# The first words tile on GpSimd's queue, in two halves, and decoded in front of the first exponentials

## The chip, the cores and the metric

The kernel runs on one core of one Trainium2 chip. The core has a TensorE (PE: matmuls, and the weight loads in front of them, PEld), a VectorE (DVE), a ScalarE (ACT), a GpSimd (POOL) and a SyncE (SP), which share the on-chip memory SBUF; matmuls write to PSUM. Transfers between HBM and SBUF are asked for by an engine's queue (here SP's, once ACT's) and carried by 16 DMA engines that the core's queues share. The metric is device time in microseconds. The kernel before took 1014.36 us, the median of three runs (1013.2 to 1014.84).

## The reference

Four batches of eight heads of attention with a threshold: a score below the row's maximum minus tau is dropped before the softmax. Its output goes through two feed-forward nets: the first is gated and has no nonlinearity but the product, the second has a leaky ReLU.

```
scores = q @ k.T / 8                                   # 4 x 8 heads, 576 x 576, head_dim 64
attn   = softmax(where(scores >= max(scores) - tau, scores, -1e9))
x = (attn @ v) -> 2304 x 512                           # heads side by side
x = ((x @ w1) * (x @ w2)) @ w3 @ w_out                 # w1, w2: 512 x 1024; w3: 1024 x 1024; w_out: 1024 x 512
h = x @ w_in                                           # 512 x 2048
out = maximum(0.01 * h, h) @ moe2_w_out                # 2048 x 512
```

All inputs are float32 of small magnitude.

## The kernel before

The weights reach the core as 64-bit words, whose two 32-bit columns (`low` and `high`) make one float32 value; a *half* is 512 such values in each of 128 partitions. Decoding a half (`decode`, lines 137 to 161) takes two activations on ACT (L147 on the high words into `t`, L149 on the low words into `lw`), a shift on DVE (L150) and two additions on POOL (L154). Halves that belong to w1 and w2 are also split in two parts, which takes an ACT cast (L156) and a subtraction (L158, on DVE for every second half). There are 40 halves: those of w_out and w3 come in pairs, one 1 MB transfer to a `raw` tile for two halves (L133), those of w1 and w2 singly (L127, `st`). The order is `first` (lines 406 and 407): w_out's tiles 0 and 1, w3's tile 0, w_out's 2 and 3, and so on. Called h0, h1, ... here, h0 and h1 are the first `raw` tile, h2 and h3 the second, h4 and h5 (w3's tile 0) the third, h6 and h7 the fourth.

The attention runs over 80 steps (`STEPS`). One step is a block of 128 query rows of two heads, or of 64 rows of each: `scores` (PE matmuls L262, then on DVE the negated row maximum L271 and on ACT the exponentials L272), `mask` (DVE L286, the sum's reciprocal L290 and L291, and in the first three steps a diagonal `dg` of the reciprocals, L295 on ACT and L296 on DVE), `transposes` (PE L314 or L312, copies L355 on ACT and L347 on DVE) and, once per head pair, `weighted` (PE L371, the product with V). Q is scaled in `prepare_unit` (DVE, L216) before the first scores of its head pair. Into these steps the program lays the decoding (`load_halves`), the product of w3 and w_out that is taken once (`fold_weights`, PE L420, in pieces of two matmuls given out by `fold_some`), and later, as filler on PE, the first net for the 384 tokens that are finished (`gated`, L450 and L471). The second net follows as a pure matmul stage (L909, L944).

PE's and SP's instructions stay in the order in which the program is written; ACT's, DVE's and POOL's are ordered by a scheduler that may move them, except those under `keep_in_program_order`, to which the two activations of a decode and the scaling of Q belong. Every engine works through its own list and stops at an instruction that waits. Before the first scores PE multiplies the identity with itself nine times, and ten times behind them (`keep_busy`, L527), which keeps it running until there is work; the identity is made by POOL (masks.py, lines 197 and 199).

At the start SP asks for the first head pair's K and Q (four transfers, L186 and L190), for h0 and h1 (L133), for the second pair's K and Q, for the next three `raw` tiles, and for V (L202, L203). In step 0 the program decodes h0 before `mask(0)` and h1 after its transposes, in steps 1 to 4 four halves each. The transfer of a further `raw` tile waits for one of four buffers.

Of the kernel before, what the change touches and what calls it, by code (L numbers as in the profile page):

```python
# [10 lines left out]
I32 = mybir.dt.int32  # L11
# [38 lines left out]
def attention_gated_ffn(ctx: ExitStack, tc: tile.TileContext, qkv, tau, w3t, wout, w12, w2, out):  # L50
# [6 lines left out]
    nc = tc.nc  # L57

    def f(ap):
        return ap.bitcast(F32)  # L60
# [44 lines left out]
    def stream(jobs, by_dve):  # L105

        todo = [(job, c) for job in jobs for c in range(2)]
        loaded = []
        state = [0, None]

        def issue(most=2 * len(jobs)):

            while len(loaded) < min(most, len(todo)):
                (slot, src, raw), c = todo[len(loaded)]
                if len(loaded) >= state[0] + (7 if raw else 5):
                    return
                if raw is None:
                    st = wld.tile([P, 1024], I32, tag="st", name="st", bufs=4)
                    nc.sync.dma_start(out=st, in_=src[:, c * 512:c * 512 + 512].bitcast(I32))  # L127
                    loaded.append(st)
                else:
                    if c == 0:  # L130
                        state[1] = wpool.tile(
                            [P, 2, 1024], I32, tag=raw, name="raw")
                        nc.sync.dma_start(  # L133
                            out=state[1].rearrange("p c w -> p (c w)"), in_=src.bitcast(I32))
                    loaded.append(state[1][:, c])

        def decode():
            for k, ((slot, src, raw), c) in enumerate(todo):
                if c == 0:
                    dst = slot()  # L140
                sl = slice(c * 512, c * 512 + 512)
                words = loaded[k].rearrange("p (w two) -> p w two", two=2)
                low, high = words[:, :, 0], words[:, :, 1]
                t = wld.tile([P, 512], I32, tag="t", name="t", bufs=2)
                lw = wld.tile([P, 512], I32, tag="lw", name="lw", bufs=2)
                tc.keep_in_program_order(
                    nc.scalar.activation(f(t), f(high), AF.Prelu, scale=2.0 ** -112, alpha=-2.0 ** 32))  # L147
                tc.keep_in_program_order(
                    nc.scalar.activation(lw, low.bitcast(U32), AF.Copy, scale=2.0 ** -29))  # L149
                nc.vector.tensor_scalar(  # L150
                    out=t, in0=t, scalar1=3, scalar2=None, op0=ALU.logical_shift_left)
                whole = dst[:, sl].bitcast(I32) if len(dst.shape) == 2 else lw
                for part in (slice(0, 256), slice(256, 512)):
                    nc.gpsimd.tensor_tensor(out=whole[:, part], in0=t[:, part], in1=lw[:, part], op=ALU.add)  # L154
                if len(dst.shape) == 3:
                    nc.scalar.copy(dst[:, 0, sl], f(t))  # L156
                    eng = nc.vector if by_dve and c else nc.gpsimd
                    eng.tensor_tensor(out=dst[:, 1, sl], in0=f(lw), in1=f(dst[:, 0, sl]), op=ALU.subtract)  # L158
                state[0] = k + 1
                yield  # L160
                issue()

        return decode(), issue
# [3 lines left out]
    def piece_of(u):  # L167

        b, p, g = UNITS[u]
        gq, gw, blocks = PARTS[b % 2][g]  # L170
        at = b * S + gq
        return gq, gw, blocks[0] is None, at // GW, at % GW

    def load_unit(u):

        if u >= len(UNITS):
            return
        b, p, _ = UNITS[u]
        gq, gw, _, _, _ = piece_of(u)
        h = 2 * p  # L180
        qk = apool.tile([P, KS + GW], F32, tag="qk", name="qk", bufs=3)
        for a in range(2):
            o = a * D
            src = qkv[b, h + a][o:o + D]
            if gq == 0:
                nc.sync.dma_start(out=qk[o:o + D, D:KS + gw], in_=src[:, :S + gw])  # L186
            else:
                nc.sync.dma_start(out=qk[o:o + D, D:KS], in_=src[:, :S])
                nc.sync.dma_start(out=qk[o:o + D, KS:KS + gw], in_=src[:, S + gq:2 * S])
            nc.sync.dma_start(out=qk[o:o + D, :D], in_=src[:, S - D:S])  # L190
        qk_t[u] = qk
# [49 lines left out]
    def scores(n, between=None):  # L241

        u, c = STEPS[n]
        qk = qk_t[u]
        heads = range(1 if c is None else 2)
        sc = [ps_a.tile([P, 2, 512], F32, tag=f"sc{a}", name="sc") for a in heads]
        if u < PER:
            parts, qzu = (qk,), qz.unsqueeze(1)
        else:
            parts, qzu = qks_t[u], qzs  # L250
        passes = PASSES[:1] if u < PER else PASSES
        for half in range(2):
            for i, (x, y) in enumerate(passes):
                for a in heads:
                    if c is None:
                        lhs, rhs = qzu[:, x], parts[y][:, D + half * HS:D + half * HS + HS]
                    else:
                        r = slice(a * D, a * D + D)
                        o = KS + c
                        k0 = (D, 0)[a] + half * HS  # L260
                        lhs, rhs = parts[x][r, o:o + P], parts[y][r, k0:k0 + HS]
                    nc.tensor.matmul(  # L262
                        sc[a][:, half, :HS], lhs, rhs, start=(i == 0), stop=(i == len(passes) - 1))
        if between:
            between()
        e = apool.tile([P, 2 * S], F32, tag="e", name="e", bufs=2)
        few = apool.tile([P, 6], F32, tag="nm", name="nm", bufs=4)
        nms, th = few[:, :2], few[:, 2:4]
        for a in heads:
            nm = nms[:, a:a + 1]  # L270
            nc.vector.tensor_reduce(out=nm, in_=sc[a][:, :, :HS], op=ALU.max, axis=AX.XY, negate=True)  # L271
            ex = nc.scalar.activation(  # L272
                e[:, a * S:a * S + S].rearrange("p (a b) -> p a b", a=2), sc[a][:, :, :HS], AF.Exp, bias=nm)
            if between:
                tc.keep_in_program_order(ex)
        m = len(heads)
        nc.vector.tensor_scalar(
            out=th[:, :m], in0=nms[:, :m], scalar1=-1.0, scalar2=cb, op0=ALU.mult, op1=ALU.add)
        sc_t[n], e_t[n] = (sc, [th[:, a:a + 1] for a in heads], few[:, 4:]), e
# [110 lines left out]
    def slot(table, i, tag, name):  # L390
        def make():
            if tag == "w3":
                table[i] = fold.tile([P, 1024], F32, tag=tag, name=name, bufs=3)
            elif name == "wo":
                if i % 2 == 0:
                    table["both"] = fold.tile([P, 2, 1024], F32, tag=tag, name=name, bufs=2)
                table[i] = table["both"][:, i % 2]
            else:
                table[i] = wpool.tile([P, 2, 1024], F32R, tag=tag, name=name)
            return table[i]  # L400
        return make
# [87 lines left out]
    in_order = ExitStack()  # L489
    in_order.enter_context(tc.manual_schedule(engines={mybir.EngineType.SP}))  # L490
    load_tau()
    load_unit(0)
    loads, issue = stream(first, True)
    issue(2)
    load_unit(1)
    issue()
    load_v(0)
    prepare_unit(0)
    halves_in = [0]
    folded = [0]  # L500

    def load_halves(k):
        for _ in range(k):
            if next(loads, 0) != 0:
                halves_in[0] += 1
# [17 lines left out]
    def keep_busy(k):  # L523

        scratch = ps_w.tile([P, 512], F32, tag="w", name="scratch")
        for _ in range(k):
            nc.tensor.matmul(scratch[:, :P], ident, ident, start=True, stop=True)  # L527

    folding = fold_weights()
    keep_busy(9)  # L530
    scores(0)
    keep_busy(10)
    weigh = []
# [9 lines left out]
    for n in range(NS):  # L543
        u, c = STEPS[n]
# [106 lines left out]
    def issue():  # L651
        while len(raws) < min(used[0] + 3, len(order)):
            j, c = order[len(raws)]
            st = wld.tile([P, 1024], I32, tag="st", name="st", bufs=4)
            nc.sync.dma_start(out=st, in_=w2[j, :, c * 512:c * 512 + 512].bitcast(I32))
            raws.append(st)
# [387 lines left out]
```

## Time and profile before

| | |
|---|---|
| median of three runs | 1014.36 us |
| the profiled execution, its time | 1013.22 us |
| its span, first to last instruction | 1011.3 us |
| TensorE busy | 997.3 us (99%) |
| VectorE busy | 638.8 us (63%) |
| ScalarE busy | 571.3 us (56%) |
| GpSimd busy | 242.5 us (24%) |

The span is 1.9 us shorter than the execution's own time, and that is 1.14 us under the median. TensorE is busy nearly throughout, so what it stands idle for adds to the time. The page's second part cuts the span into 40 slices of 25 us; the whole change lies in the first of them and its consequences in the first six.

### The profile page before, as it was taken

What the parts mean: (1) busy time and instruction counts of PE and PEld (TensorE: products, weight loads), DVE (VectorE), ACT (ScalarE), POOL (GpSimd) and SP (SyncE); (2) the same over time, 40 slices, a digit from 0 to 9 for tenths busy, and PEclk for the clock granted to TensorE, in tenths of its full rate; (3) what the DMA queues carried; (4) which work ended last, traced back from release to release, by engine and by line L of the source; (5) the groups of instructions that cost most, each with busy time, mean ns of one, the idle gap of its engine ahead of it and who ended that gap; (6) DMA issues with size and microseconds to landing.
All of it is one profiled execution on the core that took longest, in us unless ns stands there. A gap on an engine that the chain in (4) does not pass through costs nothing.

```text
span 1011.3 us, 16227 instructions
## 1 busy us (share of the span) xinstructions
PE 997.3 (99%) x5909; PEld 846.8 (84%) x5909; DVE 638.8 (63%) x1370; ACT 571.3 (56%) x1068; POOL 242.5 (24%) x257
## 2 busy tenths in 40 slices
PE   7999999999999999999999999999999999999998
PEld 6544578888888888888888899999989999999997
DVE  7988889887777677898877355567582111521112
ACT  5978755555655554555655354878864333543332
POOL 2755531101100110111011062454461111411110
PEclk9999999999999999999999999999999999999999
DMA  8962422141121111223101227497537951074401
GB/s 263 344 220 98 129 58 58 53 131 34 34 64 49 40 30 62 59 71 88 45 12 55 68 88 273 176 326 265 173 130 278 392 213 42 1 282 160 192 1 63
DMA packets 52271, 129.51 MB, mean 128 GB/s; under 512 B 15712, under 2 KB 30304, under 8 KB 48352
## 3 DMA queue, kind: packets, MB, share of 16 engines
q1 hardware_dynamic: 51904, 128.35, 36.7%
q8 instruction: 47, 0.77, 0.3%
q14 instruction: 32, 0.26, 0.1%
q10 hardware_dynamic: 288, 0.13, 0.0%
HBM read 95.95 MB, written 32.51 MB: 127 GB/s over the span
## 4 chain that ended last, share of the span: by engine, by line
PE 85%; DVE 9%; ACT 3%; issue 2%; DMA 1%; POOL 0%; SPq 0%; DVEq 0%; ACTq 0%; POOLq 0%
PE po L944 19%; PE psab L450 18%; PE ps L909 17%; PE psh L471 10%; PE av L371 7%; PE sc L262 6%; PE tp L312 5%; PE ps L420 3%; DVE e L286 2%; DVE nm L271 2%; DMA qk<-in_qkv 1%; DVE t L150 1%; DVE HH L347 1%; DVE e L302 1%; PE tq L312 1%
## 5 line engine op out<-in xcount | busy, mean ns | idle before, releaser
L450 PE MATMUL psab<-x,w 128*128 128x384 f32 x1152 | 234.1, 347 | 0.0
L944 PE MATMUL po<-dn,gg 128*128 128x512 f32 x864 | 222.8, 390 | 0.0
L450 PEld LDWEIGHTS psab<-x,w 128*128 128x128 f32 x1152 | 196.4, 188 | 9.7 <-issue 9.4
L944 PEld LDWEIGHTS po<-dn,gg 128*128 128x128 f32 x864 | 160.0, 188 | 22.0
L909 PE MATMUL ps<-h,uph 128*128 128x384 f32 x672 | 172.8, 338 | 1.1 <-DVE sum L891 0.6
L891 DVE TENSOR_TENSOR sum<-snap,ps 128x384 f32<-128x384 f32 x72 | 39.8, 552 | 172.3 <-PE ps L909 156.5
L909 PEld LDWEIGHTS ps<-h,uph 128*128 128x128 f32 x672 | 123.5, 188 | 15.1 <-DVE sum L891 1.4
L272 ACT ACTIVATE e<-sc,nm 128x576 f32<-128x576 f32 x144 | 100.6, 739 | 62.7 <-DVE nm L271 62.1
L286 DVE SCALAR_TENSOR_TENSOR e<-sc,nm,e 128x576 f32<-128x576 f32 x144 | 113.1, 815 | 12.9 <-ACT e L272 7.9
L271 DVE TENSOR_REDUCE nm<-sc 128x1 f32<-128x576 f32 x144 | 103.3, 751 | 28.1 <-PE sc L262 28.0
L464 POOL TENSOR_TENSOR gt<-at,gt 128x384 fp32r<-128x384 f32 x46 | 47.5, 1033 | 299.4 <-ACT gt L462 299.4
L471 PE MATMUL psh<-gt,w 128*128 128x384 f32 x576 | 116.0, 346 | 0.0
L909 PE MATMUL ps<-h,upl 128*128 128x384 f32 x336 | 113.1, 337 | 0.0
L899 POOL TENSOR_TENSOR gg<-sum,gg 128x384 fp32r<-128x384 f32 x48 | 50.4, 1049 | 251.8 <-ACT gg L898 237.5
L471 PEld LDWEIGHTS psh<-gt,w 128*128 128x128 f32 x576 | 98.3, 188 | 6.3 <-issue 6.3
L886 ACT COPY snap<-ps 128x384 f32<-128x384 f32 x72 | 34.3, 476 | 89.4 <-PE ps L909 89.4
L312 PE MATMUL tp<-ident,e 128*128 128x128 f32 x488 | 73.8, 274 | 0.9 <-ACT HH L355 0.2
L312 PEld LDWEIGHTS tp<-ident,e 128*128 128x128 f32 x488 | 59.5, 140 | 17.5 <-issue 7.2
L371 PE MATMUL av<-HH,vv 128*64 128x384 f32 (+1 forms) x512 | 67.7, 407 | 0.5 <-DVE HH L347 0.5
L347 DVE COPY HH<-tp 128x512 f32<-128x512 f32 x64 | 43.7, 683 | 36.3 <-PE tp L312 36.1
L896 ACT ACTIVATE sum<-sum 128x384 f32<-128x384 f32 x72 | 37.8, 526 | 48.2 <-DVE sum L891 48.2
L909 PEld LDWEIGHTS ps<-h,upl 128*128 128x128 f32 x336 | 63.1, 188 | 0.0
(125 smaller groups left out, 1419.2 us busy)
## 6 DMA issues: line engine op xcount, KB each, us to landing
st<-in_w SPq DMA_DIRECT2D x48, 512.0 KB, 5.0
dn<-dn_d SPq DMA_DIRECT2D x10, 1024.0 KB, 7.2
uph<-up_d SPq DMA_DIRECT2D x10, 896.0 KB, 8.9
upl<-up_d SPq DMA_DIRECT2D x10, 896.0 KB, 4.7
raw<-in_w3t SPq DMA_DIRECT2D x8, 1024.0 KB, 9.6
vv<-in_qkv SPq DMA_DIRECT2D x64, 128.0 KB, 2.2
dn_d<-dn SPq DMA_DIRECT2D x8, 1024.0 KB, 6.5
up_d<-uph SPq DMA_DIRECT2D x8, 896.0 KB, 4.7
```

Source lines behind the costliest of these rows:

```text
L262: nc.tensor.matmul(sc[a][:, half, :HS], lhs, rhs, start=(i == 0), stop=(i == len(passes) - 1))
L271: nc.vector.tensor_reduce(out=nm, in_=sc[a][:, :, :HS], op=ALU.max, axis=AX.XY, negate=True)
L272: ex = nc.scalar.activation(e[:, a * S:a * S + S].rearrange("p (a b) -> p a b", a=2), sc[a][:, :, :HS], AF.Exp, bias=nm)
L286: nc.vector.scalar_tensor_tensor(out=ev, in0=sc[a][:, :, :HS], scalar=th, in1=ev, op0=ALU.is_ge, op1=ALU.mult, accum_out=st[:, a:a + 1])
L312: nc.tensor.transpose(out, part, ident)
L347: nc.vector.tensor_copy(HH[:, :, a, o:o + P], tp)
L371: nc.tensor.matmul(av[a * D:a * D + D, :gw], vv[:, a, kc], rhs, start=(i == 0), stop=(i == NK - 1))
L450: nc.tensor.matmul(ps, w12_t[i][:, a, mat * 512 + kk * P:mat * 512 + kk * P + P], xt[kk][:, c], start=(m == 0), stop=(m == 11))
L471: nc.tensor.matmul(ps, w34_t[i // 2][:, a, i % 2, o * P:o * P + P], gt[i][:, c], start=(m == 0), stop=(m == 23))
L899: eng.tensor_tensor(out=gg[:, 1], in0=gf, in1=f(gg[:, 0]), op=ALU.subtract)
L909: nc.tensor.matmul(ps, (uph, upl)[a][:, wi, i * P:i * P + P], hs[k][:, c, i], start=(opens[k] and m == 0), stop=(m == 5), skip_group_check ...
L944: nc.tensor.matmul(po_t[o], gg[:, c, t * P:t * P + P], dn[:, i, a], start=(q == 0 and seen[o] == 1 and m == 0), stop=(q == NQ - 1 and seen ...
```

## The change

The first `raw` tile (h0 and h1, 1 MB) is no longer asked for by SP in one transfer but by POOL in two of 512 KB each, and at the head of its program: `issue(2)` stands in front of `load_unit(0)`. Two halves are decoded (`load_halves(2)`) between the nine and the ten identity products, ahead of the first scores in the program. From there the decoding is two halves ahead of what it was at each place, with as many halves per step as before.

```diff
@@ in stream(), issue() @@
                     if c == 0:
                         state[1] = wpool.tile(
                             [P, 2, 1024], I32, tag=raw, name="raw")
-                        nc.sync.dma_start(
-                            out=state[1].rearrange("p c w -> p (c w)"), in_=src.bitcast(I32))
+                        words = src.bitcast(I32)
+                        if loaded:
+                            nc.sync.dma_start(out=state[1].rearrange("p c w -> p (c w)"), in_=words)
+                        else:
+                            for i in range(2):
+                                nc.gpsimd.dma_start(out=state[1][:, i], in_=words[:, i * 1024:i * 1024 + 1024])
@@ the start of the program @@
     load_tau()
-    load_unit(0)
     loads, issue = stream(first, True)
     issue(2)
+    load_unit(0)
     load_unit(1)
     issue()
     load_v(0)
...
     keep_busy(9)
+    load_halves(2)
     scores(0)
     keep_busy(10)
```

The lines of the changed kernel are four to five higher from `decode` on: its L151, L153, L154 and L158 are the L147, L149, L150 and L154 of before, its L220 is L216, L276 is L272, L299 is L295.

DVE at the start of the program, before: `scl` and `cb` come from tau, `qk` is Q, `sc` the scores, `t` the shifted words.

```order
L102 TENSOR_TENSOR cb<-cb,neg 128x1
L216 TENSOR_SCALAR qk<-qk,scl 128x384
L271 TENSOR_REDUCE nm<-sc 128x1 x2
L277 TENSOR_SCALAR nm<-nm,cb 128x2
L286 SCALAR_TENSOR_TENSOR e,nm<-sc,nm,e 128x576 x2
L150 TENSOR_SCALAR t<-t 128x512
L290 TENSOR_SCALAR nm<-nm 128x2
L291 RECIPROCAL nm<-nm 128x2
L296 TENSOR_SCALAR dg<-ident,nm 128x128
```

The same place on DVE in the changed kernel:

```order
L102 TENSOR_TENSOR cb<-cb,neg 128x1
L154 TENSOR_SCALAR t<-t 128x512
L220 TENSOR_SCALAR qk<-qk,scl 128x384
L154 TENSOR_SCALAR t<-t 128x512
L275 TENSOR_REDUCE nm<-sc 128x1 x2
L281 TENSOR_SCALAR nm<-nm,cb 128x2
L290 SCALAR_TENSOR_TENSOR e,nm<-sc,nm,e 128x576 x2
L154 TENSOR_SCALAR t<-t 128x512
L294 TENSOR_SCALAR nm<-nm 128x2
L295 RECIPROCAL nm<-nm 128x2
L300 TENSOR_SCALAR dg<-ident,nm 128x128
```

The shift of h0 now stands in front of the scaling of Q and that of h1 in front of the first row maximum; the shift behind `mask(0)`'s two products, which was h0's, is now h2's.

ACT at the start of the program, before (`raw` is the words tile, `dg` the diagonal, `tp` the transposed block):

```order
L95 DMA tauc<-in_tau 128x1
L272 ACT_TABLE_LOAD
L272 ACTIVATE e<-sc,nm 128x576 x2
L147 ACTIVATE t<-raw 128x512
L149 ACTIVATE lw<-raw 128x512
L295 ACTIVATE dg<-ident,nm 128x128
L272 ACTIVATE e<-sc,nm 128x576 x2
L355 COPY HH<-tp 128x4x128
```

The same place on ACT in the changed kernel:

```order
L95 DMA tauc<-in_tau 128x1
L151 ACT_TABLE_LOAD
L151 ACTIVATE t<-raw 128x512
L153 ACTIVATE lw<-raw 128x512
L151 ACTIVATE t<-raw 128x512
L153 ACTIVATE lw<-raw 128x512
L276 ACTIVATE e<-sc,nm 128x576 x2
L151 ACTIVATE t<-raw 128x512
L153 ACTIVATE lw<-raw 128x512
L299 ACTIVATE dg<-ident,nm 128x128
L276 ACTIVATE e<-sc,nm 128x576 x2
L359 COPY HH<-tp 128x4x128
```

Four activations (h0 and h1) now stand in front of the first exponentials, and the two in front of `dg` read h2, which is in the second `raw` tile.

POOL at the start of the program in the changed kernel, where before nothing stood between the two instructions that make the identity (`masks.py`):

```order
L1038 MEMSET const-bfloat16-1.0 128x1
L1038 MEMSET const-uint8-127 128x1
L1046 UNCONDITIONAL_BRANCH
masks.py:197 MEMSET ident 128x128
L138 DMA raw<-in_wout 128x1024 x2
masks.py:199 ISA
masks.py:199 AFFINE_SELECT ident<-ident 128x128
L158 TENSOR_TENSOR wo<-t,lw 128x256 x8
```

The two DMA issues have come between the clearing of the identity and the instruction that sets its ones.

## Rows read from the trace of the kernel before

**Rows 1.** The page's first part: busy time, share of the span, instructions.

```profile
PE 997.3 (99%) x5909; PEld 846.8 (84%) x5909; DVE 638.8 (63%) x1370; ACT 571.3 (56%) x1068; POOL 242.5 (24%) x257
```

**Rows 2.** Windows: busy time and instructions of each engine by stretch.

```profile
core 0: us, PE busy (x) PEld busy (x) DVE busy (x) ACT busy (x) POOL busy (x), PEclk, DMA share, GB/s
0.00:5.00 5.00, 3.64 (x18) 3.61 (x18) 1.47 (x9) 1.28 (x1) 0.70 (x6) 1.00 0.59 126
5.00:10.00 5.00, 3.86 (x30) 3.16 (x28) 2.70 (x5) 1.64 (x3) 0.00 (x0) 1.00 0.94 297
...
25.00:30.00 5.00, 4.01 (x16) 2.33 (x16) 4.95 (x10) 5.00 (x10) 3.36 (x5) 1.00 0.99 398
50.00:55.00 5.00, 5.00 (x15) 2.49 (x16) 5.00 (x8) 5.00 (x10) 4.43 (x6) 1.00 1.02 366
55.00:60.00 5.00, 4.26 (x24) 1.76 (x24) 4.96 (x13) 3.99 (x8) 3.14 (x4) 1.00 0.15 30
```

**Rows 3.** PE's waits, 0 to 160 us: us in total, times, longest.

```profile
PE scratch L527 <- POOL ident masks.py:199: 1.4, 1, 1.4
PE ps L420 <- POOL w L154: 1.3, 1, 1.3
PE sc L262 <- DVE qk L216: 1.1, 1, 1.1
PE tq L332 <- ACT xr L375: 0.9, 1, 0.9
```

**Rows 4.** Timeline, 0 to 30 us: start, duration, engine, line.

```profile
1.01 0.29 POOL masks.py:199 TENSOR_SCALAR_AFFINE_SELECT ident<-ident 128x128 f32<-128x128 f32 x1
...
1.36 3.80 PE L527 MATMUL scratch<-ident 128*128 128x128 f32 x18 [1.36 <-POOL ident masks.py:199]
...
3.26 0.59 SPq L133 DMA_DIRECT2D raw<-in_wout  x1
...
5.82 0.42 DVE L216 TENSOR_SCALAR qk<-qk,scl 128x384 f32<-128x384 f32 x1 [1.82 <-DMA qk<-in_qkv]
...
6.30 1.31 PE L262 MATMUL sc<-qk 64*128 64x288 f32 x8 [1.14 <-DVE qk L216]
...
7.54 2.50 PE L527 MATMUL scratch<-ident 128*128 128x128 f32 x20
...
7.57 1.42 DVE L271 TENSOR_REDUCE nm<-sc 128x1 f32<-128x576 f32 x2 [1.33 <-PE sc L262]
8.36 1.41 ACT L272 ACTIVATE e<-sc,nm 128x576 f32<-128x576 f32 x2 [5.94 <-DVE nm L271]
...
9.21 0.33 SPq L202 DMA_DIRECT2D vv<-in_qkv  x1
...
10.85 0.42 DVE L150 TENSOR_SCALAR t<-t 128x512 int32<-128x512 int32 x1
11.19 0.16 DVE L290 TENSOR_SCALAR nm<-nm 128x2 f32<-128x2 f32 x1
...
13.95 0.47 SPq L203 DMA_DIRECT2D vv<-in_qkv  x1
...
16.68 0.67 ACT L147 ACTIVATE t<-raw 128x512 f32<-128x512 f32 x1
...
17.38 0.43 DVE L150 TENSOR_SCALAR t<-t 128x512 int32<-128x512 int32 x1 [0.55 <-ACT t L147]
```

**Rows 5.** SP's own waits, 0 to 40 us, the two for w_out's words.

```profile
SPq L203 <- DMA raw<-in_wout: 3.3, 2, 2.1
...
SPq L202 <- DMA raw<-in_wout: 1.2, 1, 1.2
```

**Rows 6.** DMA, 0 to 30 us: what the engines moved in 40 slices of 0.75 us.

```profile
GB/s 0 0 16 98 285 257 220 175 393 393 385 268 238 254 320 404 437 415 415 448 415 448 415 361 346 341 38 18 118 227 143 274 80 339 382 393 404 393 415 426
```

**Rows 7.** Timeline of DVE, 23 to 62 us: a wait for PE, and a split.

```profile
41.23 0.69 DVE L347 COPY HH<-tp 128x512 f32<-128x512 f32 x1 [0.26 <-PE tp L312]
...
56.37 0.68 DVE L158 TENSOR_TENSOR w<-lw,w 128x512 fp32r<-128x512 f32 x1
```

## The prediction

> **What bounds the kernel now.** I read the page's first part, then the windows, then PE's waits, then the first 30 us of the timeline. TensorE is busy for 997.3 of 1011.3 us [rows 1], so its own work is nearly the whole time, and a change that leaves that work as it is can only move the rest, 14.0 us. The windows show where some of it is: PE stands idle for 1.36 us in the first 5 us, 1.14 in the next five, 0.99 from 25 to 30 and 0.74 from 55 to 60 [rows 2]. The waits name causes: the identity (1.4), the scaling of Q (1.1), POOL's decoded w3 (1.3), ACT's copy at L375 later on (0.9) [rows 3]. The reader is to see two more things. In the first 10 us DVE and ACT are mostly idle (4.17 and 2.92 us busy, the first two rows added): that is the room into which the change decodes. From 25 us on DVE is full (4.95, 5.00 and 4.96 of 5 us) and ACT nearly so [rows 2]: there a delay from the front is not made up. In the front there is one chain: Q lands, DVE scales it at 5.82, scores at 6.30, row maximum at 7.57, exponentials at 8.36 [rows 4]. What enters this chain costs its full length.
>
> **What the change does to the front.** No arithmetic is added or removed; two halves are decoded earlier. But the order puts the shift of h0 on DVE before the scaling of Q. Q, row maxima and all that DVE does are queued behind it, and PE's scores wait for Q. So the scaling starts at the later of Q's landing and h0's landing + 0.70 (from the activation at 16.68 to the shift at 17.38) + 0.34 (from the shift at 10.85 to the next at 11.19) [rows 4]. To be no later than 5.82, h0 must land by 4.78.
>
> When does it land? The trace has no transfer from POOL, so I bound it. Two queues share the engines: at the full rate of 0.393 MB/us that the slices from 6.0 to 7.5 us show [rows 6], first Q and K (0.52 MB) and h0 (0.52 MB) need 2.6 us from 2.25, where the rate picks up, thus 4.9. A transfer is seen as landed some time after its bytes: the second words tile's 3.14 MB (Q and K twice, two tiles) are counted by about 12.8 [rows 6], and SP, which waited for it [rows 5], goes on at 13.95 [rows 4], so 1.1 later. Together 6.0. Bounds: 1.0 (POOL's identity begins at 1.01, the issues now in its place) + 0.59 (an issue on SP [rows 4]) + 1.3 (0.52 MB at that rate) + 1.1 = 4.0 from below; from above the first words tile of now, asked for at 3.26, lets SP go on at 9.21 [rows 4, 5]. I take 6.0. Scaling then starts at 7.04, 1.2 us late. h1, with the second Q and K beside it, needs 2.65 us more, 8.65; its shift 9.35, the row maximum 9.7 in place of 7.57, 2.1 late. The exponentials start at 10.5 and end at 11.9.
>
> *The skill's price.* The Trainium skill (DMA: Bandwidth & Descriptors, section on the anatomy of one SWDGE DMA) fits 2.0 us + bytes/436e3 to a transfer asked for by GpSimd. By it, as an estimate, h0 would land at 1.0 + 3.2 = 4.2 and hold up nothing; it is for a transfer by itself. No run here shows one yet.
>
> *The skill's warning.* The slices show 0.098 to 0.285 MB/us before 5.25 us [rows 6], so engines have room early. The Trainium skill (SBUF — State Buffer, section on SBUF's two separate sides) says that GpSimd cannot write its DMA descriptors while VectorE runs certain operations that take their shared port. VectorE is busy for 1.47 us of the first five [rows 2]; by that rule, as an estimate, h0 would come up to 1.5 us later than without it, 7.5 in place of 6.0. No row here decides it.
>
> **The third half.** This is the term that I take to decide. Behind the exponentials ACT now decodes h2, where before it had h0. h2 lies in the second words tile. `dg`, the next exponentials and DVE's shift and reciprocals are queued behind that. Now this tile is there at 13.9, and the half before h2 is decoded at 16.68 only [rows 4], so nothing shows. In the changed kernel it is wanted at 11.9. Its bytes come behind the same 2.1 MB. At full use: Q and K twice, 1.05 MB at 0.26 (the slices from 8.25 to 10.5 [rows 6]), 4.0 us, and two tiles, 2.1 MB at 0.40, 5.25 us, make 9.25 from 2.25 on, thus 11.5, and 1.1 to land: 12.6. With a little lost early, I take 12.7; the bounds are 10.9 (all at 0.415) and 13.9 (as now). Then the shift comes at 12.7 + 0.70 = 13.4 instead of 10.85: 2.55 late. The 2.1 from the front lie within that; they alone decide if the tile is there before 12.3.
>
> **What is given back.** Later decoding runs two halves ahead at an equal number per step, so steps 1 to 4 carry the load they had. The wait of PE for w3 (1.3) goes, since h4 moves from the second part of step 1 to the first, ahead of that step's exponentials. But behind it DVE and ACT are full; DVE itself waits for PE at 41.23 by 0.26 only [rows 7]. I count 0.26, and up to 1.3 if PE is what counts. The first split of w1 and w2 also comes two halves earlier, into the full stretch before the stop at 55 to 60: one more subtraction on DVE, +0.68 [rows 7]. At the other end two halves fewer are left near 130 us, which I count as the whole of PE's 0.9 there [rows 3]. One piece of the w3 product moves from step 3 to step 2 on PE, with the same work: 0, covered by DVE being the fuller engine; uncovered, PE would wait in step 3 for a copy of ACT of about 0.6.
>
> POOL's identity stands behind two issues. If one takes T, the identity products start at 1.36 + 2T and end at 5.16 + 2T. T is not in the trace; the nearest row is SP's issue, 0.59 [rows 4], and I allow up to three times that, 1.7. At 1.0, which I take, they end at 7.16, before the scores' 7.5: 0. At 1.7 they end at 8.56, 1.0 beyond, still inside the 2.55. The first 18 products' instructions take 0.211 us each and the 20 behind the scores 0.125 [rows 4], so PE reached its upper level, 2.4 GHz, after them; if it came too late for the scores, these (1.31) would take up to 1.2 longer.
>
> SP: the fourth w_out tile is now asked for before the second V and third Q and K. These wait behind it, and Q is scaled near 27 only; cost 0. SP's one issue less makes the second Q and K 0.6 earlier, contained in 12.7.
>
> **Sum.** 2.55 - 0.26 + 0.68 - 0.9 = +2.1 us. The profiled execution took 1013.22 (span 1011.3 and 1.9 around it), which makes 1015.3; against the median of the runs, 1014.36, that lies 1.14 low, so I forecast 1014.36 + 2.1 = 1016.5.
>
> **Rivals.**
> *In time (not slower).* Both of POOL's transfers and the second tile use the slices that are empty now: h0 by 4.8 and the tile at its bound of 10.9, which is 0.75 late for a shift at 10.85. For it: only 0.6 MB are moved by 5.0 us [rows 6]. Against: 4.9 for h0 by bytes alone. It costs 0.75 - 0.26 + 0.68 - 0.9 = +0.3; with PE's 1.3 returned in full and the split hidden 0.75 - 1.3 - 0.9 = -1.45, and -2.2 with the tile in time as well. Middle -0.6: 1013.8. It holds while h0 lands by 4.8 and the tile before 11.2 or so.
> *Only the front.* The 1.2 to 2.1 worked out for h0 and h1, and the second tile there when wanted: 1.7 - 0.5 = +1.2, 1015.6. For it: the queue from POOL takes no place in SP's.
> *The words come no earlier (the change doesn't do what it says).* POOL's issues or its queue are slow and h0 lands at 9.2 as now; DVE scales Q at 10.2, 4.4 late: 4.4 - 0.5 = +3.9, 1018.3; a late identity and the lower clock at the scores on top of the front reach 2.1 + 1.0 + 1.2 - 0.5 = +3.8. For it: the engines are full from 6 us on (0.393), so what isn't moved by then only displaces other words. Against: POOL asks 2.3 us earlier than SP did.
>
> **How the numbers follow.** Forecast 0.42, in time 0.15, only the front 0.20, no earlier 0.23. This kernel's measurement can't tell less than 0.2%, 2.0 us, from no change. Within the forecast, landings of the tile from 12.3 to 13.9 give +1.6 to +3.3, about six in ten of them beyond 2.0: 0.25 slower, 0.17 same. In time: 0.05 faster, 0.10 same. Only the front: 0.18 same, 0.02 slower. No earlier: 0.22 slower, 0.01 same. Sums: faster 0.05, same 0.46, slower 0.49. The range goes from half a microsecond under in time's middle to one above the last rival, 1013.3 to 1019.3; the forecast's own is 1016.0 to 1017.7.
>
> **What would show it.** Right: the first shift on DVE releases the scaling of Q near 7.0, the ACT activation of h2 waits for the second tile by about 0.8, the first `dg` comes near 14.2 instead of 11.66, PE's wait for POOL's w3 is gone, and the wait at L375 shrinks. Wrong: scaling at 5.8 to 6.0 with no wait for ACT (in time); exponentials late but no wait for the second tile (only the front); PE's first product after 4 us, or POOL's words at 9 us (no earlier). If the front is late by 2.5 and the whole time isn't, a stretch that I took for full has absorbed it.

## The result

The changed kernel takes 1021.4 us, the median of six runs (1019.62 to 1022.63); the kernel before, run beside it, 1013.65 (six runs, 1013.2 to 1014.84). The ratio is 1.0069, with a 95% interval of 1.0058 to 1.008: it is slower by some 7 us. Forecast were 1016.5 (2.1 slower) and a range up to 1019.3. The direction was right, the size was more than three times too small.

### The profile page after: what moved, and what is told of

Read it like the earlier page. It is cut to its first block, busy times and chain, and to the rows that moved or that the text cites. A ratio compares the mean times of both kernels' runs of the same rounds, so it can differ in the third digit from the quotient of the medians.

```text
span 1019.0 us, 16232 instructions
## 1 busy us (share of the span) xinstructions
PE 999.4 (98%) x5909; PEld 849.9 (83%) x5909; DVE 639.5 (63%) x1370; ACT 572.4 (56%) x1068; POOL 243.4 (24%) x259
## 3 DMA queue, kind: packets, MB, share of 16 engines
q0 software_dynamic: 288, 1.05, 0.3%
## 4 chain that ended last, share of the span: by engine, by line
PE 88%; DVE 5%; ACT 3%; issue 1%; DMA 1%; SPq 0%; DVEq 0%; ACTq 0%
PE psab L454 19%; PE po L950 19%; PE ps L915 17%; PE psh L475 10%; PE av L375 7%; PE sc L266 7%; PE tp L316 5%; PE ps L424 3%; DVE e L290 1%; DMA qk<-in_qkv 1%; ACT t L151 1%; DVE nm L275 1%; PE tq L316 1%; DVE t L154 1%; PE tp L335 1%
## 5 line engine op out<-in xcount | busy, mean ns | idle before, releaser
L915 PEld LDWEIGHTS ps<-h,uph 128*128 128x128 f32 x672 | 123.5, 188 | 15.4 <-DVE sum L897 1.7
L276 ACT ACTIVATE e<-sc,nm 128x576 f32<-128x576 f32 x144 | 100.8, 738 | 59.6 <-DVE nm L275 59.4
L375 PE MATMUL av<-HH,vv 128*64 128x384 f32 (+1 forms) x512 | 67.6, 406 | 0.5 <-DVE HH L351 0.5
```

The costliest lines, as they stand in the source:

```text
L276: ex = nc.scalar.activation(e[:, a * S:a * S + S].rearrange("p (a b) -> p a b", a=2), sc[a][:, :, :HS], AF.Exp, bias=nm)
L375: nc.tensor.matmul(av[a * D:a * D + D, :gw], vv[:, a, kc], rhs, start=(i == 0), stop=(i == NK - 1))
L915: nc.tensor.matmul(ps, (uph, upl)[a][:, wi, i * P:i * P + P], hs[k][:, c, i], start=(opens[k] and m == 0), stop=(m == 5), skip_group_check ...
```

## The profile after

The profiled execution took 1021.1 us, its span is 1019.0, so 7.7 above that of before. The page's first part, in answer to [rows 1]:

```profile
PE 999.4 (98%) x5909; PEld 849.9 (83%) x5909; DVE 639.5 (63%) x1370; ACT 572.4 (56%) x1068; POOL 243.4 (24%) x259
```

The same 5909 matmul instructions keep PE busy for 2.1 us longer. The windows say why (columns as in [rows 2]; the granted clock is the third figure from the end):

```profile
0.00:5.00 5.00, 2.04 (x9) 2.04 (x10) 1.47 (x9) 1.28 (x1) 1.94 (x8) 1.00 0.48 110
5.00:10.00 5.00, 2.07 (x11) 1.87 (x9) 0.48 (x2) 1.22 (x2) 1.40 (x2) 1.00 1.08 280
10.00:15.00 5.00, 4.58 (x15) 3.25 (x16) 2.79 (x6) 2.55 (x4) 1.40 (x2) 0.53 1.02 345
15.00:20.00 5.00, 5.00 (x33) 4.40 (x33) 3.66 (x10) 2.10 (x5) 1.40 (x2) 0.79 1.03 413
...
45.00:50.00 5.00, 2.95 (x19) 1.86 (x18) 4.50 (x9) 4.09 (x10) 2.38 (x3) 1.00 0.75 212
...
60.00:65.00 5.00, 3.79 (x15) 1.61 (x13) 5.00 (x10) 4.80 (x9) 3.94 (x5) 1.00 0.29 88
65.00:70.00 5.00, 3.61 (x25) 1.80 (x26) 4.85 (x11) 3.37 (x7) 2.98 (x4) 1.00 0.00 0
```

PE stands idle for 5.89 us in the first ten (2.50 in the kernel before) and then, from 10 to 15 us, works at a granted clock of 0.53, so nearly all of the time at 1.2 GHz, the lower level. Two stretches with idle time are new: 2.05 at 45 to 50 and 2.60 at 60 to 70. PE's waits of the first 160 us answer to [rows 3]:

```profile
PE sc L266 <- DVE qk L220: 3.4, 1, 3.4
PE tp L316 <- ACT HH L359: 3.3, 2, 2.0
PE scratch L532 <- POOL ident masks.py:199: 3.0, 1, 3.0
PE tp L318 <- ACT HH L359: 2.5, 2, 1.7
PE av L375 <- ACT tl L357: 1.4, 1, 1.4
```

The waits for POOL's w3 and for ACT's copy `xr` (L375 of the kernel before) are gone, as forecast. The largest is now the wait for the scaled Q. The timeline of the front answers to [rows 4]:

```profile
1.28 1.23 POOL L138 DMA_DIRECT2D raw<-in_wout  x2 [0.34 <-issue]
...
2.96 4.11 PE L532 MATMUL scratch<-ident 128*128 128x128 f32 x18 [2.96 <-POOL ident masks.py:199]
...
6.74 0.66 ACT L151 ACTIVATE t<-raw 128x512 f32<-128x512 f32 x1 [4.31 <-DMA raw<-in_wout]
...
7.43 0.43 DVE L154 TENSOR_SCALAR t<-t 128x512 int32<-128x512 int32 x1 [3.35 <-ACT t L151]
...
9.94 0.42 DVE L220 TENSOR_SCALAR qk<-qk,scl 128x384 f32<-128x384 f32 x1 [2.08 <-DMA qk<-in_qkv]
10.42 3.15 PE L266 MATMUL sc<-qk 64*128 64x288 f32 x8 [3.35 <-DVE qk L220]
10.93 0.66 ACT L151 ACTIVATE t<-raw 128x512 f32<-128x512 f32 x1 [2.96 <-DMA raw<-in_wout]
...
13.50 4.19 PE L532 MATMUL scratch<-ident 128*128 128x128 f32 x20
13.53 1.61 ACT L276 ACTIVATE e<-sc,nm 128x576 f32<-128x576 f32 x2 [1.39 <-DVE nm L275]
...
15.50 0.67 ACT L151 ACTIVATE t<-raw 128x512 f32<-128x512 f32 x1 [0.36 <-DMA raw<-in_wout]
...
16.96 0.40 ACT L299 ACTIVATE dg<-ident,nm 128x128 f32<-128x128 f32 x1 [0.22 <-DVE nm L295]
```

h0 is there at 6.74, where SP's whole tile came at 9.21 before. But Q is scaled at 9.94, not at 5.82, and what ended DVE's wait was Q's own transfer: the shift of h0 had been done 2.08 us earlier. The scores take 3.15 us in place of 1.31, the products behind them 4.19 in place of 2.50. h2, the term that the forecast rested on, holds ACT up by 0.36 only. The DMA engines from 5 to 6.5 us, one line for a queue: packets, MB, share of the 16 engines' time (q0 is POOL's, q1 SP's):

```profile
q0 software_dynamic: 140, 0.51, 100.3%
q1 hardware_dynamic: 49, 0.02, 4.2%
```

For this stretch POOL's words have the engines nearly to themselves, and the second head's K and Q, asked for by SP between 2.0 and 3.2, stand nearly still. The slices of 0.75 us over the first 30 us answer to [rows 6]:

```profile
GB/s 0 0 16 82 202 284 276 316 380 339 214 213 199 215 261 291 340 404 448 415 415 448 393 448 367 414 385 450 404 334 304 221 166 183 57 88 284 470 382 470
```

The engines move somewhat more from 4.5 to 7.5 us than before (0.276 to 0.380 MB/us), but it is other bytes.

## The experiments

Each ran beside the kernel before, whose median was 1014.50 us for four of them (transfer alone, decoding alone, ACT's queue, words when Q has landed), 1014.39 for the next four (only h0 on POOL, asks one step earlier, Q over two queues, 26 products) and 1014.51 for the last four. Delays of `dg`, the first diagonal, are against its 11.66 of before.

### One half of the change at a time

The transfer alone: the changed kernel without the early decoding.

```diff
     keep_busy(9)
-    load_halves(2)
     scores(0)
```

> The words' two transfers stay on POOL's queue, the decoding goes back to where it was before (no two halves ahead of the first scores). Theory (POOL's 1 MB goes ahead of Q on the shared DMA engines; Q lands at 9.9 instead of 5.8, TensorE falls to 1.2 GHz while it waits, the first scores take 3.15 and the second step's come late): Q is scaled at 9.9 again, the first scores run at the lower clock, and the time is 1018.5 to 1020.5, nearly the whole of the 7.7 us. Rival (the decode order: DVE's shift in front of the scaling, the third half's words): Q lands when it did, time 1013 to 1015.

Measured: 1019.69 us, ratio 1.0057 (1.0042 to 1.0072), as the theory had it. Its row of the scaling in the timeline:

```profile
10.03 0.42 DVE L220 TENSOR_SCALAR qk<-qk,scl 128x384 f32<-128x384 f32 x1 [5.94 <-DMA qk<-in_qkv]
```

No shift stands in front of it here, and DVE waits for Q all the same. So Q's lateness is the transfer's doing, not the order's.

The decoding alone: the kernel before, with two halves decoded in front.

```diff
     keep_busy(9)
+    load_halves(2)
     scores(0)
```

> The kernel before, its transfers unchanged on SP's queue, with two halves decoded ahead of the first scores. Theory (the transfer is the cause): Q is scaled at 5.8 and the first scores end at 7.6 at the upper clock; what remains is that ACT's exponentials stand behind the words, which land at 9.2, and h2 behind the second tile at 13.9: the first dg about 15.4 instead of 11.7, thus up to +3.7, time 1016 to 1018. Rival (the decode order costs it all): 1020 to 1022.

Measured: 1021.06 us, ratio 1.0066 (1.0049 to 1.0083). The range of the theory, 1016 to 1018, was missed; the time lies in the rival's. Its timeline:

```profile
5.82 0.42 DVE L216 TENSOR_SCALAR qk<-qk,scl 128x384 f32<-128x384 f32 x1 [1.83 <-DMA qk<-in_qkv]
...
11.07 0.66 ACT L147 ACTIVATE t<-raw 128x512 f32<-128x512 f32 x1 [8.64 <-DMA raw<-in_wout]
...
13.29 1.36 ACT L272 ACTIVATE e<-sc,nm 128x576 f32<-128x576 f32 x2
...
15.07 2.99 PE L262 MATMUL sc<-qk 64*128 64x288 f32 x8 [5.04 <-DVE e L286]
```

Q is in time, but ACT stands at h0 until 11.07, the exponentials start at 13.29 instead of 8.36, and PE waits 5.04 and then works at the lower level (granted clock 0.50 from 15 to 20 us; 2.99 for scores that took 1.94). I had taken 9.2 for h0. The same ask, at 3.26, lands 1.9 us later here than in the trace of before (9.21); why, no row shows, and so it is open how much of the delay is the order's. Each half of the change alone costs nearly what both cost together, and `dg` comes at 16.38 (transfer), 16.18 (decoding) and 16.96 (both): the two delays lie beside each other, they do not add.

### Is it POOL's queue, or any early transfer?

The words on ACT's queue, at the same place.

```diff
-    nc.gpsimd.dma_start(out=state[1][:, i], in_=words[:, i * 1024:i * 1024 + 1024])
+    nc.scalar.dma_start(out=state[1][:, i], in_=words[:, i * 1024:i * 1024 + 1024])
```

> The changed kernel with the two words transfers asked for on ACT's queue in place of POOL's, decode order as in the changed kernel. Theory A (a transfer of POOL's goes ahead of SP's on the engines, 81% to 17% of their time from 3.3 to 6.3 us; one of ACT's shares evenly): Q lands at 7.5 to 8.5, time 1016.5 to 1019. Theory B (any second queue of 1 MB pushes Q back as far): Q at 9.5 to 10.5, time 1020 to 1022.

Measured: 1020.52 us, ratio 1.0061 (1.0046 to 1.0076), theory B's range.

```profile
10.11 0.42 DVE L220 TENSOR_SCALAR qk<-qk,scl 128x384 f32<-128x384 f32 x1 [2.18 <-DMA qk<-in_qkv]
```

h0 at 6.80, Q at 10.11: the same on another queue, so Q's delay isn't due to GpSimd's way of issuing.

Only h0 on POOL, h1 on SP behind the first K and Q, the decoding as before:

```diff
-    nc.gpsimd.dma_start(out=state[1][:, i], in_=words[:, i * 1024:i * 1024 + 1024])
+    (nc.gpsimd, nc.sync)[i].dma_start(out=state[1][:, i], in_=words[:, i * 1024:i * 1024 + 1024])
...
-    issue(2)
     load_unit(0)
+    issue(2)
...
     keep_busy(9)
-    load_halves(2)
```

> As e1_transfer_only, but only h0's 512 KB are asked for by POOL at the head of the program, h1's by SP behind the first K and Q. Theory (order of asking): half as much stands ahead of Q, which is scaled at 7.5 to 8.3 in place of 10.0; time 1015.5 to 1018. Rival (a second queue costs Q its share whatever its size): Q at 9.5 or later, 1019 or more.

Measured: 1016.32 us, ratio 1.0018 (1.0009 to 1.0027); the time and Q's scaling are as expected.

```profile
7.90 0.42 DVE L220 TENSOR_SCALAR qk<-qk,scl 128x384 f32<-128x384 f32 x1 [3.80 <-DMA qk<-in_qkv]
8.37 1.31 PE L266 MATMUL sc<-qk 64*128 64x288 f32 x8 [1.70 <-DVE qk L220]
```

Half the bytes ahead of Q make Q half as late: 2.08 us for 0.52 MB, 4.1 to 4.2 for 1.05 MB, both 0.25 MB/us, close to what the engines carry of Q and K alone (0.257 to 0.285 [rows 6]). So in these runs Q's delay goes with the bytes that are asked for beside it.

The words asked for by POOL when Q has landed (POOL first copies a column of Q into the tile, which makes it wait), decoding as before:

```diff
+    nc.gpsimd.tensor_copy(state[1][:, i, :1].bitcast(F32), qk_t[0][:, KS:KS + 1])
     nc.gpsimd.dma_start(out=state[1][:, i], in_=words[:, i * 1024:i * 1024 + 1024])
...
-    issue(2)
     load_unit(0)
+    issue(2)
...
     keep_busy(9)
-    load_halves(2)
```

> As e1_transfer_only, but POOL first copies one column of the landed Q into the words tile, so that it asks for the words only once Q is there. Theory (it is the early 1 MB that pushes Q back): Q is scaled at 5.8 to 6.0, the clock is up at the first scores, time 1013 to 1015. Rival (POOL's queue itself, or the identity behind its issues, costs the time wherever the transfer stands): above 1017.

Measured: 1020.83 us, ratio 1.0064 (1.0049 to 1.0079), so the theory's 1013 to 1015 was missed. POOL asks at 6.53, among the three tiles, 3 MB, for which SP asks from 5.83 to 6.93, and h0 is there at 16.36. The DMA queues from 8 to 10 us and the ACT row:

```profile
q1 hardware_dynamic: 78, 0.64, 89.8%
```

```profile
16.36 0.66 ACT L152 ACTIVATE t<-raw 128x512 f32<-128x512 f32 x1 [5.07 <-DMA raw<-in_wout]
```

The mirror image: here POOL's queue moves nothing for two microseconds, while SP's tiles move. Q was nearly in time (6.29), and the words paid. The time lies in the rival's range, above 1017; against the rival, POOL's queue itself, speaks the next run.

The asks one step earlier, when the first head's K and Q are there:

```diff
-    nc.gpsimd.tensor_copy(state[1][:, i, :1].bitcast(F32), qk_t[0][:, KS:KS + 1])
+    nc.gpsimd.tensor_copy(state[1][:D, i, :1].bitcast(F32), qk_t[0][:D, KS:KS + 1])
```

> As e5_words_behind_q, but POOL waits only for the first head's K and Q, so that it asks for the words at about 5 us, behind all four transfers of the first pair and ahead of SP's next 3 MB of words; the decode order is that of before. Theory (the engines serve transfers nearly in the order in which they are asked for, whatever the queue): Q is scaled at 5.8 to 6.3, the words land at 8.5 to 10.5 against 16.4 in e5_words_behind_q, time 1013 to 1015.5. Rival (POOL's queue is served late or takes what it gets at any time): words after 12 us or Q after 7, time above 1017.

Measured: 1014.33 us, ratio 1.0000 (0.9991 to 1.001). Its timeline:

```profile
5.25 1.28 POOL L139 DMA_DIRECT2D raw<-in_wout  x2 [0.19 <-POOL raw L138]
...
5.99 0.42 DVE L221 TENSOR_SCALAR qk<-qk,scl 128x384 f32<-128x384 f32 x1 [1.98 <-DMA qk<-in_qkv]
...
6.47 2.36 PE L267 MATMUL sc<-qk 64*128 64x288 f32 x8 [0.89 <-DVE qk L221]
```

With the asks behind Q's and ahead of SP's next tiles, the words on POOL's queue cost no time. They win nothing either. That is a balance: the scores take 2.36 in place of 1.31 and `dg` comes 1.15 later, while PE's wait for w3 falls from 1.3 to 0.2. Of the words, h0 came when expected (some 10.5), h1 not (some 15.4, 9.5 us from its ask).

Q spread over two queues: the kernel before, with the second head's K and Q of the first pair asked for by ACT.

```diff
-    nc.sync.dma_start(out=qk[o:o + D, D:KS + gw], in_=src[:, :S + gw])
+    eng = nc.scalar if u == 0 and a else nc.sync
+    eng.dma_start(out=qk[o:o + D, D:KS + gw], in_=src[:, :S + gw])
```

> The kernel before with the first pair's second K and Q asked for on ACT's queue beside SP's, words and decoding as before. Theory (Q's landing is set by the order and the time of asking; four asks in a row on SP take 2.5 us): Q is scaled at 4.5 to 5.0 in place of 5.8, each later step of the front comes 0.7 to 1.2 earlier, time 1012.5 to 1013.5 against 1014. Rival (Q's bytes and landing set it, or the words come too late for the step): 1013.7 to 1015.

Measured: 1016.65 us, ratio 1.0018 (1.001 to 1.0027), a miss for all my numbers. Q is scaled at 6.24, later than 5.82: SP, with fewer asks, comes to the words tile at 1.99 instead of 3.26, and from 5 to 6.5 us its queue has 86.0% of the engines' time, ACT's 10.1%. But 0.42 us of delay aren't the 1.8 that the ratio shows. The larger part is PE's own work:

```profile
6.72 3.12 PE L264 MATMUL sc<-qk 64*128 64x288 f32 x8 [1.15 <-DVE qk L218]
9.77 4.58 PE L529 MATMUL scratch<-ident 128*128 128x128 f32 x20
```

These took 1.31 and 2.50 before; PE's idle time in the first 160 us, 8.34, is no longer than before (8.50). The granted clock reads 1.00 all the while, and why PE was slower here no row shows.

### The clock, and the later order

26 in place of 9 identity products in the changed kernel, so that PE runs until Q is scaled:

```diff
-    keep_busy(9)
+    keep_busy(26)
     load_halves(2)
```

> The changed kernel with 26 identity products in place of 9 ahead of the first scores, so that TensorE works while it waits for Q. Theory (the clock's fall to 1.2 GHz while TensorE waits for Q costs about 1.8 us in the scores and 1.7 in the products behind them): the granted clock stays 1.00 from 10 to 20 us, the first scores take 1.3 to 1.9; but dg of step 0 still waits for h2's words, so only what the second scores were late by is won: 1.0 to 2.5 us less than the changed kernel, 1019 to 1020.5. Rival (the clock only shows what waits anyway): no change, 1021 to 1022.

Measured: 1020.98 us, ratio 1.0058 (1.0045 to 1.0072). The scores are fast again (1.24 us, 1.9 less), but a window further on reads:

```profile
40.00:50.00 10.00, 7.98 (x41) 3.88 (x39) 9.06 (x18) 9.08 (x18) 6.25 (x9) 0.93 0.61 191
```

The idle time of 2.02 there is as in the changed kernel, and the clock now falls in this stretch (0.91, 0.92, 0.93 and 0.90 in the four from 20 to 60). The expectation, at least 1.0 us less than the changed kernel, was missed: it is 0.4 by the medians, and the ranges of the two overlap.

The changed kernel with nothing decoded in step 0, so that from step 1 on the decoding stands where it was:

```diff
-    kh = 4 if 0 < n < 5 else 3 if 6 < n < 10 else 2
+    kh = 0 if n == 0 else 4 if n < 5 else 3 if 6 < n < 10 else 2
```

> The changed kernel, but step 0 decodes nothing, so that from step 1 on the decoding is where the kernel before has it; the front is the changed kernel's. Theory (Q's late landing and the words ahead of the exponentials hold up the front, and the two-halves-ahead order costs something of its own later): Q scaled at 9.9 as in the changed kernel, but dg(0) released by the exponentials without h2, near 15 to 16 in place of 16.96, and PE's waits at 45 to 50 and 60 to 70 us (2.05 and 2.6 there) shrink to under 1.5 together: 1018.5 to 1020.5. Rival (what is late in front only passes through, the later order costs nothing): the later idle time stays within half a microsecond and the time at 1021 to 1022.

Measured: 1019.28 us (1019.01 to 1020.46), ratio 1.0046 (1.0031 to 1.0061).

```profile
45.00:50.00 5.00, 4.99 (x24) 2.65 (x23) 4.71 (x9) 4.60 (x10) 2.56 (x4) 1.00 0.88 285
60.00:65.00 5.00, 4.26 (x24) 1.85 (x24) 4.97 (x12) 4.14 (x8) 3.32 (x4) 1.00 0.30 63
65.00:70.00 5.00, 5.00 (x26) 2.28 (x21) 4.86 (x11) 3.92 (x7) 3.12 (x4) 1.00 0.19 53
```

The idle time at 45 to 70 is 0.75 in place of 4.65, though Q is scaled at 9.95 as in the changed kernel; the waits for POOL's w3 (1.7) and `xr` (0.9) are back. Over the first 160 us PE's idle time is 11.40 in place of 13.92. `dg` is only 0.23 earlier (16.73, expected were 15 to 16), so little of this comes from the front. By the medians the later order costs 2.1 us; the two intervals overlap a little. The front is slow here too, but at another granted clock:

```profile
10.43 3.06 PE L266 MATMUL sc<-qk 64*128 64x288 f32 x8 [3.26 <-DVE qk L220]
```

```profile
10.00:15.00 5.00, 4.57 (x16) 3.39 (x17) 2.89 (x6) 2.65 (x4) 1.40 (x2) 1.00 1.01 352
```

Both together:

```diff
-    keep_busy(9)
+    keep_busy(26)
...
-    kh = 4 if 0 < n < 5 else 3 if 6 < n < 10 else 2
+    kh = 0 if n == 0 else 4 if n < 5 else 3 if 6 < n < 10 else 2
```

> The changed kernel with 26 in place of 9 identity products in front of the first scores (PE runs until Q is there) and with nothing decoded in step 0. Theory (three terms: Q's landing 4.1, the slower clock behind the wait, the later order): only the first is left, 1014.4 + 4.1 less what the fuller stretches give back, 1017 to 1018.5, with the clock at 1.00 in the first 20 us. Rival (the clock is not a term of its own, since the words hold up the exponentials anyway): the same time as without the longer identity products, within 0.7 us of the run that only leaves step 0 empty.

Measured: 1018.44 us (1018.29 to 1018.94), ratio 1.0035 (1.0021 to 1.0049). PE's timeline:

```profile
2.97 8.20 PE L532 MATMUL scratch<-ident 128*128 128x128 f32 x52 [2.97 <-POOL ident masks.py:199]
11.10 1.28 PE L266 MATMUL sc<-qk 64*128 64x288 f32 x8
```

0.84 us under the run that only leaves step 0 empty, and their ranges do not meet. So PE's slower work behind the wait (scores of 3.06 in place of 1.28, products of 3.13 in place of 2.50) is a term of its own, but a small one: the rival's bound was 0.7, which four runs of each can't tell from 0.84, and 0.15 of it is Q's earlier landing. That it is the clock the granted clock does not show, since it reads 1.00 in both runs. What is left, 3.9 us over the kernel before by the medians (3.6 by the ratio), is about Q's delay of 3.98 (9.80 here).

### Can the change be had without its cost?

The kernel with late asks that cost nothing, and the two halves decoded in front:

```diff
     keep_busy(9)
+    load_halves(2)
     scores(0)
```

> The changed kernel's decoding order, but POOL asks for the two halves only when the first head's K and Q are there (5.2 us), with which Q lands at 6.0. Theory (the decoding order is a cause by itself): Q scaled near 6.0, but the exponentials stand behind words that land near 9.5 to 10.5, so they start at 12 to 13.3 in place of 8.36 and the time is 1017.5 to 1021. Rival (the transfer is the only cause, decoding early is harmless once Q is in time): 1013.5 to 1015.

Measured: 1024.95 us, ratio 1.0099 (1.0085 to 1.0113), beyond the expected range. Its timeline:

```profile
10.26 0.66 ACT L152 ACTIVATE t<-raw 128x512 f32<-128x512 f32 x1 [7.83 <-DMA raw<-in_wout]
...
15.14 0.66 ACT L152 ACTIVATE t<-raw 128x512 f32<-128x512 f32 x1 [3.66 <-DMA raw<-in_wout]
...
17.99 2.99 PE L267 MATMUL sc<-qk 64*128 64x288 f32 x8 [7.80 <-DVE e L291]
```

I had put both halves near 10. h1 shares the engines with SP's next tiles and comes at 15.14; everything stands behind it.

Late asks, the order of before and 13 identity products:

```diff
-    keep_busy(9)
+    keep_busy(13)
```

> The words on POOL's queue, asked for behind the first head's K and Q, the decoding order of the kernel before, and 13 in place of 9 identity products, so that PE does not stand idle before Q is scaled. Theory (without these products that kernel lost at the slower clock what PE's wait for POOL's w3 gave back): scores at 6.5 in 1.31 in place of 2.36 us, the products behind them 2.50 in place of 3.56, dg 1 earlier than 12.81, 1012.5 to 1014. Rival (what counts in step 0 is DVE and ACT, not PE): 1014 to 1015.

Measured: 1013.71 us, ratio 0.9997 (0.9988 to 1.0005). `dg` comes at 12.43, 0.4 earlier than without the further products, not 1. The median lies in the theory's range, but no difference from the kernel before can be told, so no version here beats it.

## Why the prediction was wrong

**The step that failed** is "first Q and K (0.52 MB) and h0 (0.52 MB) need 2.6 us from 2.25", and what was drawn from it. I used it for h0's landing only and left Q's where it was: scaling at "the later of Q's landing and h0's landing", with 5.82 as the first of the two. Yet the engines were not idle while Q landed, and the "room early" that I read from the slices was none. The engines' busy share in the slices of [rows 6], in tenths, in the kernel before:

```profile
DMA  0015999599999999999999989911667949999999
```

From 3.0 to 5.25 us they are busy for at least 90% and carry 0.220 to 0.285 MB/us, not the 0.393 that I took for the full rate. h0's shift was done by 7.9; Q came at 9.94. Bytes account for most of it: the changed kernel's slices sum to 1.58 MB by 8.25 us (1.03 on POOL's queue, 0.55 on SP's), which is Q and K (0.52) with nearly *all* of the words (1.05), and the 1.1 us to landing that I had used make 9.35. The last 0.6 are open.

**The terms, one by one.** h0 at 6.0: 6.74. POOL's issue at 1.0: 0.62; the identity products end at 7.07 (7.16 forecast) and hold up nothing. h1 at 8.65: 10.93, but it decides nothing either, since the row maximum waits for the scores. The third half, +2.55: the second tile lands later than I took, near 15.5 (12.7), but the exponentials end then too, so it adds 0.36; the term is void. Given back: PE's waits for w3 and `xr` went as forecast. Of the clock I had said "up to 1.2 longer" at the scores, on the condition that the identity came late; the scores were longer behind the wait for Q instead, by 1.84, and the products behind them by 1.69, of which the time shows 0.4 to 0.8 (26 products, with and without the later order). That PE reached 2.4 GHz only after its first 18 products I had taken from their durations; the granted clock reads 1.00 over both stretches [rows 2]. The copy that I counted as 0, or "about 0.6" if uncovered, was a wait of 2.05: step 3's transposes have no piece of the w3 product between them now, and ACT does other work from 45.02 on and comes to the copy at 47.20. DVE was not the cover that I took it for. The split, 0.68, stands in a stretch whose idle time rose by 1.9 (2.60 at 60 to 70, 0.74 at 55 to 60 before).

**The sum that should have been.** By the experiments, 3.9 for Q, 0.8 for PE's slower work behind the wait and 2.1 for the later order make 6.8, beside 7.0 by the ratio. These are steps from one kernel to the next, so they must add up; what speaks for them is that the first is the size of Q's delay (3.98) and that PE's idle time falls by 2.5 with the last. By the two traces: PE's idle time in the first 160 us went from 8.5 to 13.9, its busy time up by 2.1, together 7.5 of the span's 7.7. The sum of the windows over 160 us, after:

```profile
sum 160.00, PE 146.08 PEld 91.11 DVE 131.65 ACT 113.00 POOL 76.92; mean PE 14.61 PEld 9.11 DVE 13.16 ACT 11.30 POOL 7.69
```

And before:

```profile
sum 160.00, PE 151.50 PEld 94.44 DVE 137.82 ACT 115.98 POOL 77.24; mean PE 15.15 PEld 9.44 DVE 13.78 ACT 11.60 POOL 7.72
```

**The rivals.** *The words come no earlier* gave the nearest time, 1018.3, with scaling at 10.2, for the wrong reason, which is luck: h0 came 2.5 us earlier (h1 1.7 later), and Q paid. Its argument, that whatever isn't moved early "only displaces other words", was the right one, had I asked what else is displaced. *In time* and *Only the front* fell with Q.

**What held.** A delay from the front is for the most part not made up. In the runs that decode as before from step 1 on, `dg` later by 1.6, 2.1, 4.6, 4.7, 5.1 and 6.1 us came with +1.8, +1.8, +3.6, +5.8, +4.7 and +6.5 us of time by the ratios (Q on two queues; half on POOL; both terms out; transfer alone; none in step 0; words when Q has landed). Only the 1.2 and 0.8 of the late asks came with no longer time. In the five with two halves in front throughout, the time is 0.9 to 2.6 more than the delay: 4.5, 4.9, 5.3, 5.3 and 7.4 came with +6.7, +5.9, +6.2, +7.0 and +10.0 (decoding alone; 26 products; ACT's queue; changed; late asks with early decoding). That is what the later order costs behind the front.

*The rule that was missed.* The Trainium skill (DMA: Bandwidth & Descriptors, section on issuing engines that are not separate DMA queues) says that transfers of all issuing engines run on the same 16 DMA engines, so that asking from several saves issue time alone. The three runs with words on a second queue agree: Q at 9.94, 10.03 and 10.11. I weighed that page's price for GpSimd's transfer and not this rule, which speaks against the change. Its price, a fit per transfer by which h0 needs an estimated 3.2 us from the ask, was not reached in company; here it took 5.5.

## What to carry to other kernels

A transfer asked for earlier, on POOL's queue or on ACT's, was paid for here by those in flight at that time; before moving one, list what lands in that stretch, add the bytes, and give the delay to the one that the chain waits for. Early decoding in front of a chain is free only if its words land before the chain needs its engines: in order of program, a wait that an engine takes early is taken by all behind it. Price both delays apart and take the later; and follow the moved work to the full stretch behind, where it took some 2 us more here.

## What was not expected of the hardware

Two queues did not get equal parts. From 5 to 6.5 us of the changed kernel POOL's queue had 100.3% of the engines' time and SP's 4.2%; with the words on ACT's queue (q10) it was much the same:

```profile
q10 hardware_dynamic: 131, 0.47, 94.6%
q1 hardware_dynamic: 77, 0.02, 5.2%
```

From 8 to 10 us, with the words asked for when Q has landed, SP's had 89.8% and POOL's no line. The Trainium skill (DMA: Bandwidth & Descriptors, section on queues, rings and completion order) says that an engine takes turns between queues packet by packet. From 3.3 to 5 us of the changed kernel this fits (71 packets of POOL, 86 of SP, with 0.29 and 0.15 MB); in the other two stretches of POOL's it does not (140 to 49, none to 78). Part of the difference in time is the packets' size: SP's 49 hold 0.02 MB, POOL's 140 hold 0.51. Whether a queue with no line had packets ready and was passed over, or had none ready yet, no run shows.

How fast PE works stays open. Behind a wait of 3.35 us, in the changed kernel, its scores took 3.15 us and the granted clock was 0.53 from 10 to 15 us; with 26 products in front they took 1.24 at 1.00. But with nothing decoded in step 0, behind a wait of 3.26, they took 3.06 at a granted clock of 1.00; with late asks, behind an idle time of 0.89, 2.36 at 1.00; and in the kernel before, behind 1.14, 1.31 at 1.00. So the granted clock alone does not give these durations, and what decided there no row shows. Why the clock fell later in the run with 26 products isn't known either.
